# DeltaNet and SwiGLU feed-forward on one core: Q turned by VectorE, a merge on four column groups, a planner with transfer lanes

## The chip, the cores and the metric

The kernel runs on one core of a Trainium2 chip. The metric is the device time of one execution in microseconds; the time before is the median of three runs, 712.82 us (711.55 to 713.73).

A core has five engines that run their own instruction streams in order and meet at semaphores: TensorE (PE; its weight loads are listed as PEld), VectorE (DVE), ScalarE (ACT), GpSimd (POOL) and SyncE (SP). SP issues nearly all transfers (DMAs) here, in the order in which they are written; if one has to wait, all behind it wait. Matmuls write to PSUM, eight banks of 128 x 512 fp32.

## The reference

A DeltaNet recurrence over 768 steps with 4 batches x 8 heads of width 48, followed by a normalized SwiGLU feed-forward block on 3072 tokens of width 384. Everything is fp32; the weights of the block arrive as 8-byte floats.

```python
def _attn_ref(q, k, v, beta):              # q, k, v: 4, 8, 768, 48
    k_n = k / (np.linalg.norm(k, axis=-1, keepdims=True) + 1e-06)
    state = np.zeros((B, H, D, D), dtype=np.float32)
    for t in range(S):
        y[:, :, t] = np.einsum('bhd,bhde->bhe', q[:, :, t], state)
        v_old = np.einsum('bhde,bhd->bhe', state, kt)
        state = state + bt[:, :, :, None] * np.einsum('bhd,bhe->bhde', kt, vt - v_old)
...
def _moe_ref(x, w_gate, w_val, w_out, rms_g):   # x: 3072, 384; 1536 hidden
    rms = np.sqrt(np.mean(x * x, axis=-1, keepdims=True) + 1e-06)
    xn = x / rms * rms_g
    g = xn @ w_gate
    silu = g * (1.0 / (1.0 + np.exp(-g)))
    val = xn @ w_val
    return silu * val @ w_out
```

## The kernel before

**Chunks.** The 768 steps are cut into 12 chunks of 64 (C). In a chunk the recurrence is written as matmuls: a triangular system of 64 x 64 for each of the 32 pairs of batch and head is inverted, and the inverse is applied to V less what the state predicts. The inverse is made as two halves of 32 (W), which are then merged. After that the 256 tokens of the chunk go through the feed-forward block.

**The work on one chunk c**, by function and line:

- `load` (493): transfers of K, Q and V into `k2`, `q2` and `vt`. Q comes as two transfers, one for each parity g of the head, each 64 steps x 16 heads x 48 numbers. `q2` is a single buffer of 128 x 16 x 64, of which 48 columns are loaded and 16 are zero; it is filled again for the next chunk once the turn has read it.
- `norms` (551): the lengths of K's rows (line 557 on VectorE, line 560 on GpSimd).
- `prep` (583): K is scaled (629) and turned (`turn`, 508: eight transposes on TensorE, line 515, and two copies out of PSUM, line 525 or 527); K's scores (`scores`, 529, matmul at line 538) are copied (637), sent to DRAM and back in another layout (`dkk`, `at_`), scaled (654), and the two half inverses are built in 15 steps on VectorE (701 and 707). They go to DRAM and back (`dx`, `dxt`; into `mt`, `x2bd`, `m1bd`), and two merges on TensorE make the block that joins the halves: `merge1` (780, matmul at 783) and `merge2` (802, matmul at 807). The copies out of the second merge (821 on ScalarE, in chunk 0 one at 823 on VectorE) complete `mt`.
- `qpart` (568): Q is turned in the same way into `qt`, Q's scores against K are made (538) and masked into `pt` (578).
- `recur` (826): the state is applied to K and Q (848), `mt` to the rest of V (894), then `pt` (908) and K (945) to the result; the outcome is normalized and turned (1016, 1020) into `xf` for the feed-forward block. The new state is added at line 1047.
- The feed-forward block: for chunks 0 and 1 `ffn_plain` (1072; gate and value matmuls at 1083, down at 1065), in halves of the hidden width, since the weights are still arriving. From chunk 2 on `ffn` (1163) with 15 products of blocks in the place of 18 (1176) whose weights are sums made once by `factors` (1129) and `out_factors` (1202), and `down` (1214, matmul at 1233). VectorE adds products at 1186, ScalarE copies them at 1188 and takes SiLU at 1192, VectorE multiplies at 1193.

**The weights** come as 8-byte floats in 18 transfers through three buffers and are converted on ScalarE (465) and VectorE (453, 456, 461, 486); three of them are summed on TensorE (478, 479).

**The second merge** writes eight products of a 128 x 32 weight with a 128 x 128 moving tile. In the code before, the half batch bb picks the column group of the array (rows 0 or 64 of the output) and (g, p) picks 128 columns:

```python
for g in range(2):
    for p in range(2):
        for bb in range(2):
            x_ = 2 * g + p
            nc.tensor.matmul(
                ps2[bb].t[64 * bb : 64 * bb + W, 128 * x_ : 128 * x_ + 128], ...
```

An fp32 matmul stands as two records in the trace, a transpose as one.

**The order of the work** isn't the order of the code. Every step is handed to a planner (`Plan`, 63) as an operation with an engine, an estimated duration, what it reads and writes, a priority from its due time, and the PSUM banks that it takes. `forward` (111) simulates the five engines: among all operations that could start, the one with the earliest start goes first, then the one with the lowest key. A transfer occupies its issuing engine for `dur` and then one shared server for `work`. `backward` (186) makes new keys from the latest start that each operation could have, and `run` (214) repeats both 60 times with small random shifts and keeps the shortest plan, whose order is then written out engine by engine. Until planned time 70 us TensorE's gaps are filled with unneeded matmuls on `ident` (1333). A flag `after` holds a transfer back until a planned time; for Q it is 0.0, 27.2 and, from chunk 2 on, 53.2.

Of the kernel before, what the change touches and what calls it, by code (L numbers as in the profile page):

```python
# [18 lines left out]
C = 64  # L19
W = 32  # L20
# [42 lines left out]
class Plan:  # L63
# [3 lines left out]
    def __init__(self):  # L67
        self.ops, self.wrote, self.read, self.slack, self.lead = [], {}, {}, 0.0, 0.0
        self.rows = 128
        self.late = False  # L70

    def add(self, eng, dur, fn, prio, r=(), w=(), lat=0.15, ps=(), last=(), size=0):
        ps, last = ((t,) if isinstance(t, Group) else tuple(t) for t in (ps, last))
        deps = set()
        for key in r:
            if key in self.wrote:
                deps.add(self.wrote[key])
        for key in w:
            if key in self.wrote:
                deps.add(self.wrote[key])  # L80
            deps.update(self.read.get(key, ()))
        ahead = self.lead if eng == "PE" else 0.0
# [4 lines left out]
        op.size = size  # L87
# [12 lines left out]
        return op  # L100

    def first_priorities(self):
        for op in reversed(self.ops):
            if op.late:
                op.prio = min(
                    (u.prio - (0.0 if u.eng == op.eng and not op.dma else op.lat + u.slack + 0.2) for u in op.users),
                    default=op.prio,
                ) - STRETCH[op.eng] * op.dur - (3.0 if op.dma else 0.0)
            op.key = op.prio - op.ahead

    def forward(self, banks, until):
# [11 lines left out]
        order, server, end_, mode = [], 0.0, 0.0, 0  # L123
        backlog = 0.0
        while len(order) < len(self.ops):
            best = None
            for e in ENGINES:
                for op in cand[e]:
                    s = max(op.at, at[e])
                    if op.port:  # L130
                        s = max(s, held["POOL" if e == "DVE" else "DVE"])
# [41 lines left out]
            if op.dma:  # L173
                server = max(end + 0.9, server) + op.work
                end = server
            op.end = end
            for u in op.users:
# [36 lines left out]
    def run(self, free, filler=None, until=0.0):  # L214
# [4 lines left out]
        for k in range(ROUNDS):  # L219
            order = self.forward([t for t, _ in free], until if filler else 0.0)  # L220
            if order is None:
                break
            self.ends.append(self.end)
            if best is None or self.end < best[0]:
                best = self.end, [(op, op.start) for op in order]
            self.backward()
            for op in self.ops:
                op.key += SHAKE * (k % 3) * rng.uniform(-1.0, 1.0)
        self.end = best[0]
# [20 lines left out]
def kernel(  # L250
# [57 lines left out]
    k2 = sbt("k2", [128, 16, DP], NK)  # L308
    q2 = sbt("q2", [128, 16, DP])
    vt = sbt("vt", [128, 16, D])  # L310
    ksum = sbt("ksum", [128, 16], 2)
# [53 lines left out]
    def dma(dst, src, prio, r=(), w=(), work=0.3, dur=0.5, eng="SP", after=0.0):  # L365
        queue = nc.scalar if eng == "ACT" else nc.sync
        op = P.add(eng, dur, lambda: queue.dma_start(out=dst, in_=src), prio, r, w, lat=0.7)
        op.dma, op.work, op.ready = True, work, after

# [7 lines left out]
    def setup():  # L377
# [32 lines left out]
        for i in range(2):  # L410
            P.add("POOL", 1.0, lambda t=mt[i]: nc.gpsimd.memset(t, 0.0), 1, w=[("mt", i, h_, bb) for h_ in range(3) for bb in range(2)] + [("mt", i, h_, bb, g) for h_ in range(2) for bb in range(2) for g in range(2)])

# [80 lines left out]
    def load(c, what):  # L493
        t0 = c * C
        pk, pq, pv = ((-5, 1, 12), (5, 29, 36))[c] if c < 2 else (due(c, 150), due(c, 99), due(c, 70))
        for key, t, src, pr in (("k2", k2[c % NK], k, pk), ("q2", q2, q, pq)):
            for g in range(2):
                if key[0] not in what:
                    continue
                dst = t[64 * g : 64 * g + 64, :, 0:D]  # L500
                s = src.rearrange("b (y g) t e -> g t (b y) e", g=2)[g, t0 : t0 + C]
                dma(dst, s, pr, w=[(key, c % NK if key == "k2" else 0, g)], dur=0.7, work=1.02, eng="ACT" if c == 0 and g and key == "k2" else "SP", after=((0.0, 1.4, 0.0), (8.6, 27.2, 0.0))[c]["kqv".index(key[0])] if c < 2 else 53.2)
        if "v" in what:
# [79 lines left out]
    def prep(c):  # L583
# [210 lines left out]
        else:  # L794
# [4 lines left out]
            ), pi, r=[ps1], w=[("yn", 0)], last=ps1)  # L799
        ps2 = [Group(), Group()]  # L800

        def merge2():
            for g in range(2):
                for p in range(2):
                    for bb in range(2):
                        x_ = 2 * g + p
                        nc.tensor.matmul(  # L807
                            ps2[bb].t[64 * bb : 64 * bb + W, 128 * x_ : 128 * x_ + 128],
                            zz[:, 2 * bb + p, g],
                            x2bd[:, 4 * g + 2 * bb + p].rearrange("p y t -> p (y t)"),  # L810
                        )

        P.rows = 32
        P.add("PE", 0.9, merge2, pi, r=[("yn", 0)] + [("x2bd", y_) for y_ in range(4)], w=ps2 + [("mt", imt, 2, bb) for bb in range(2)], ps=ps2, size=32)
        P.rows = 128
        for bb in range(2):
            s = slice(64 * bb, 64 * bb + W)
            dst = mt[imt][s, :, W:C]
            src = lambda s=s, bb=bb: ps2[bb].t[s].rearrange("p (x t) -> p x t", t=W)
            if c or bb:  # L820
                P.add("ACT", A(512), lambda dst=dst, s=src: nc.scalar.copy(dst, s()), pi, r=[ps2[bb]], w=[("mt", imt, 2, bb)], last=ps2[bb])
            else:
                P.add("DVE", V(512), lambda dst=dst, s=src: nc.vector.tensor_copy(out=dst, in_=s()), pi, r=[ps2[bb]], w=[("mt", imt, 2, bb)], last=ps2[bb])


    def recur(c):
# [6 lines left out]
        sk = [("st", g) for g in range(2)]  # L833
        mtk = [("mt", imt, i, bb, g) for i in range(2) for bb in range(2) for g in range(2)] + [("mt", imt, 2, bb) for bb in range(2)]
        ptk = [("pt", d) for d in range(2)]
# [236 lines left out]
    def ffn_plain(c, f0, f1, start):  # L1072
# [3 lines left out]
        def up(f):  # L1076
            ps = Group()
            h_, i_, n = f // 6, f % 6 // 2, 128 * (f % 2)
            for side, key in enumerate(("wg", "wv")):
# [7 lines left out]

                P.add("PE", 1.31, mm, start + 3.9 * (f - f0), r=xk + [("wuse", h_)] + ready[(key, h_, i_)], w=[ps, (("sil", f % 2), ("hf", f, 0))[side]], ps=ps, size=12)
            a = f % 2
# [3 lines left out]
        def down(f):  # L1093
            if f == f0:
                P.add("PE", 0.0, lambda: None, start, r=xk + [("cvp", n, x_) for n in range(NPE) for x_ in range(2)], w=["po"], ps=po[1])
            P.add("PE", 1.31, down_mm(po, f, f0, f1), start + 3.9 * (f - f0) + 9, r=[("hf", f, 0), ("hf", f, 1), "wouse"] + ready[("wo", f)], w=["po"], ps=po[0], size=8)
# [66 lines left out]
    def ffn(c, start):  # L1163
        n = 0
        for h in range(2):
            ps = [Group() for _ in range(3)]
            for m, ((kind, slot), xs, b_, begin, o, more_, end) in enumerate(PRODUCTS):
# [13 lines left out]
                first = ["acq"] if m < 3 else []  # L1181
                P.add("PE", 0.9, mm, start + 0.95 * n, r=["xc", ("xp", 0), ("xp", 1), ("wx", h)], w=[g] + first, ps=g, size=16)
                n += 1
# [18 lines left out]
    def out_factors():  # L1202
        b = lambda i, j: wo_sb[:, 6 * i : 6 * i + 6, 192 * j : 192 * j + 192]
        wk = [key for f in range(FT) for key in ready[("wo", f)]]
        old = [(n_, i, d) for n_, i in (("kka", 1), ("kkb", 2)) for d in range(2)] + [("xs", 0), ("xs", 1)] + [("mt", 1, h_, bb) for h_ in range(3) for bb in range(2)] + [("mt", 1, h_, bb, g) for h_ in range(2) for bb in range(2) for g in range(2)]
        for n, (dst, in0, in1) in enumerate((
# [80 lines left out]
    load(1, "k")  # L1287
    P.slack, P.lead = 0.0, 1000.0
    norms(0)
    prep(0)  # L1290
    qpart(0)
    norms(1)
    load(1, "q")
    for c in range(NCH):
        for part_ in (recur, prep):
# [5 lines left out]
            else:  # L1301
                P.slack, P.lead = 0.0 if c < 1 else 0.1, 1000.0
                recur(c)
        P.slack, P.late = 1.0, True
        if c + 2 < NCH:
# [63 lines left out]
```

## Time and profile before

| | |
|---|---|
| median of three runs | 712.82 us |
| span of the profiled execution | 709.8 us |
| instructions on TensorE, VectorE, ScalarE, GpSimd | 10040, 1138, 732, 140 |
| second-largest share of the chain of waits: VectorE | 5% |
| bytes moved | 54.66 MB in 210,070 packets |
| filler matmuls, line 1333 | 28.0, 11.6 and 8.3 us by shape |
| Q's transfers | 24, to landing 3.7 us (median) |
| mt's transfers | 84 from SP, 32 KB each, to landing 2.2 us (median) |

The profiled execution's own time isn't recorded beside its span: the span runs from the first to the last instruction of this one execution, and the runs were timed without a profile, so 712.82 - 709.8 = 3.02 us is taken as what lies around it. Durations in the profile are per instruction, in ns for single ones. A matmul's duration is its way through the pipeline, several of which overlap, so what a group takes from TensorE is read from the distance between starts, or from the chain of waits, where each piece ends at the start of the next.

### The profile page before, as it was taken

What the parts mean: (1) busy time and instruction counts of PE and PEld (TensorE: products, weight loads), DVE (VectorE), ACT (ScalarE), POOL (GpSimd) and SP (SyncE); (2) the same over time, 40 slices, a digit from 0 to 9 for tenths busy, and PEclk for the clock granted to TensorE, in tenths of its full rate; (3) what the DMA queues carried; (4) which work ended last, traced back from release to release, by engine and by line L of the source; (5) the groups of instructions that cost most, each with busy time, mean ns of one, the idle gap of its engine ahead of it and who ended that gap; (6) DMA issues with size and microseconds to landing.
All of it is one profiled execution on the core that took longest, in us unless ns stands there. A gap on an engine that the chain in (4) does not pass through costs nothing.

```text
span 709.8 us, 23280 instructions
## 1 busy us (share of the span) xinstructions
PE 700.7 (99%) x10040; PEld 637.8 (90%) x10040; DVE 543.5 (77%) x1138; ACT 314.0 (44%) x732; POOL 139.9 (20%) x140
## 2 busy tenths in 40 slices
PE   8999999999999999999999999999999999999997
PEld 5657868778799999999999999999999999999997
DVE  4899989999679759849969769669679547957373
ACT  5435554233245445445444445346345345245241
POOL 4201211103133132233223133133213003000000
PEclk9999999999999999999999999999999999999999
DMA  7878795341451161162542431442430350040000
GB/s 138 221 149 188 180 262 170 51 79 24 75 112 27 33 111 31 28 111 46 90 77 47 74 71 25 90 76 48 78 67 11 56 103 2 15 64 2 23 1 23
DMA packets 210070, 54.66 MB, mean 77 GB/s; under 512 B 199216, under 2 KB 202288, under 8 KB 209968
## 3 DMA queue, kind: packets, MB, share of 16 engines
q1 hardware_dynamic: 205120, 52.26, 36.9%
q10 hardware_dynamic: 4848, 0.92, 0.8%
q8 instruction: 79, 1.29, 0.8%
q14 instruction: 23, 0.19, 0.1%
HBM read 40.83 MB, written 12.32 MB: 75 GB/s over the span
## 4 chain that ended last, share of the span: by engine, by line
PE 91%; DVE 5%; DMA 3%; issue 1%; ACT 1%; POOL 0%; ACTq 0%; POOLq 0%; DVEq 0%
PE bank L1176 39%; PE bank L1233 19%; PE bank L1083 9%; PE bank L1065 4%; PE bank L538 3%; PE bank L848 3%; PE bank L515 3%; PE bank L1333 2%; PE bank L894 2%; PE bank L908 2%; DMA more<-in_moe_w_gate_dram 2%; PE bank L807 2%; DVE acc L707 1%; PE bank L1016 1%; PE bank L945 1%; DVE acc L701 1%
## 5 line engine op out<-in xcount | busy, mean ns | idle before, releaser
L1186 DVE TENSOR_TENSOR tmp<-tmp,bank 128x512 f32<-128x512 f32 x180 | 121.2, 682 | 79.5 <-PE bank L1176 68.5
L1176 PE MATMUL bank<-xf,w_in 128*128 128x128 f32 x1440 | 181.1, 277 | 0.0
L1176 PEld LDWEIGHTS bank<-xf,w_in 128*128 128x128 f32 x1440 | 170.1, 192 | 2.6 <-issue 0.8
L1176 PE MATMUL bank<-xf,more 128*128 128x128 f32 x960 | 125.2, 277 | 0.0
L1176 PEld LDWEIGHTS bank<-xf,more 128*128 128x128 f32 x960 | 115.4, 192 | 2.4 <-issue 0.6
L1188 ACT COPY tmp<-bank 128x512 f32<-128x512 f32 x120 | 69.0, 586 | 78.2 <-PE bank L1176 58.3
L1192 ACT ACTIVATE tmp<-tmp 128x256 f32<-128x256 f32 x120 | 49.9, 417 | 97.9 <-DVE tmp L1186 97.6
L707 DVE TENSOR_REDUCE acc<-acc 128x30 f32<-128x90 f32 (+4 forms) x180 | 85.1, 473 | 6.2
L560 POOL TENSOR_TENSOR knrm<-ksum,half 128x16 f32<-128x16 f32 x12 | 36.2, 3019 | 158.0 <-DVE ksum L559 158.0
L701 DVE TENSOR_TENSOR acc<-acc,at 128x60 f32<-128x60 f32 (+4 forms) x180 | 62.3, 346 | 2.8
L1233 PE MATMUL bank<-wo_sb,hf 128*128 128x192 f32 x360 | 63.7, 327 | 0.0
L1233 PEld LDWEIGHTS bank<-wo_sb,hf 128*128 128x128 f32 x360 | 58.3, 190 | 0.1
L1193 DVE TENSOR_TENSOR hf<-tmp 128x256 f32<-128x256 f32 x120 | 51.0, 437 | 7.7 <-ACT tmp L1192 7.2
L1333 PE MATMUL bank<-ident 128*128 128x128 f32 (+2 forms) x160 | 44.9, 427 | 1.4 <-POOL ident masks.py:199 1.4
L728 POOL COPY acc<-acc 128x128 f32<-128x128 f32 x40 | 21.5, 568 | 123.1 <-DVE acc L707 122.5
L1333 PEld LDWEIGHTS bank<-ident 128*128 128x128 f32 x160 | 27.0, 196 | 17.9 <-issue 15.2
L654 POOL TENSOR_TENSOR at<-at,beta_b 128x1024 f32<-128x1024 f32 x8 | 18.9, 2360 | 85.7 <-DMA at<-dkk 73.7
L1083 PE MATMUL bank<-xf,w_in 128*128 128x256 f32 x144 | 34.6, 385 | 0.9 <-DVE r L862 0.9
L1065 PE MATMUL bank<-wo_sb,hf 128*128 128x384 f32 x96 | 34.6, 491 | 0.0
L1083 PE MATMUL bank<-xp,w_in 128*128 128x256 f32 x144 | 32.8, 380 | 0.0
L1083 PEld LDWEIGHTS bank<-xf,w_in 128*128 128x128 f32 x144 | 26.4, 190 | 6.0 <-DVE r L862 1.5
L1083 PEld LDWEIGHTS bank<-xp,w_in 128*128 128x128 f32 x144 | 27.0, 190 | 4.6
(166 smaller groups left out, 1024.5 us busy)
## 6 DMA issues: line engine op xcount, KB each, us to landing
at<-dkk SPq DMA_DIRECT2D x23, 256.0 KB, 4.2
q<-in_q_dram SPq DMA_DIRECT2D x24, 192.0 KB, 3.7
more<-in_moe_w_val_dram SPq DMA_DIRECT2D x6, 768.0 KB, 6.2
more<-in_moe_w_gate_dram SPq DMA_DIRECT2D x6, 768.0 KB, 7.4
more<-in_moe_w_out_dram SPq DMA_DIRECT2D x6, 768.0 KB, 6.9
vt<-in_v_dram SPq DMA_DIRECT2D x24, 192.0 KB, 4.2
out_dram<-tmp SPq DMA_DIRECT2D x48, 96.0 KB, 2.2
k<-in_k_dram SPq DMA_DIRECT2D x23, 192.0 KB, 3.8
```

The source lines that it names most:

```text
L560: P.add("POOL", 2.95, lambda: nc.gpsimd.tensor_tensor(out=knrm[i2], in0=ksum[i2], in1=half, op=ALU.pow), pn, r=[("ksum", i2), "half"], w=[ ...
L701: nc.vector.tensor_tensor(out=acc[:, 1:3, 0:n, j + 2 : W].rearrange("p a i t -> p i a t"), in0=acc[:, old, 0:n, j : j + 2, None].to_broadc ...
L707: nc.vector.tensor_reduce(out=acc[:, new, 0:n, j + 2 : W], in_=acc[:, lo : lo + 3, 0:n, j + 2 : W].rearrange("p a i t -> p i t a"), axis=A ...
L1065: nc.tensor.matmul(po[p].t[:, 0:DM], hf[:, spot(f), 128 * p : 128 * p + 128], wo_sb[:, spot(f)], start=(f == f0), stop=(f == f1 - 1), skip ...
L1083: nc.tensor.matmul(ps.t[:, TOK * side : TOK * side + TOK], w_in[:, side, h_, 3 * t + i_, n : n + 128], x_[:, 2 * t : 2 * t + 2].rearrange( ...
L1176: nc.tensor.matmul(g.t[:, 128 * z : 128 * z + 128], fac[:, side, 128 * f : 128 * f + 128], xf[:, xs], start=(begin and z == 0), stop=False ...
L1186: P.add("DVE", V(512), lambda t=t, g=g: nc.vector.tensor_tensor(out=t, in0=t, in1=g.t, op=ALU.add), -1, r=[g], w=[tk], last=g)
L1188: P.add("ACT", A(512), lambda t=t, g=g: nc.scalar.copy(t, g.t), -1, r=[g], w=[tk], last=g)
L1192: P.add("ACT", A(256), lambda t=t: nc.scalar.activation(out=t[:, 0:256], in_=t[:, 0:256], func=ACTF.Silu), -1, w=[tk])
L1193: P.add("DVE", V(256), lambda t=t, f0=f0, p=p: nc.vector.tensor_tensor(out=hf[:, spot(f0) : spot(f0) + 2, 128 * p : 128 * p + 128], in0=t[ ...
L1233: nc.tensor.matmul(g.t[:, 0:192], a_[:, f], b_[:, f], start=(begin and f == 0), stop=(f == 5), skip_group_check=True)
L1333: nc.tensor.matmul(warm[:, 0 : 128 * w_].rearrange("p (w n) -> p w n", n=128), ident, ident[:, None, :].to_broadcast([128, w_, 128]))
```

## The change

1. **Q's turn.** From chunk 2 on, Q is loaded in 16 pieces of 32 steps x 8 heads x 32 (or 16) columns, placed so that a transpose of 32 x 32 blocks gives `qt` at once. One VectorE transpose of 128 x 1024 then takes the place of eight TensorE transposes and two ScalarE copies. The loads keep the `after` time of 53.2 that the two transfers had. Chunks 0 and 1 are as before. Columns that the pieces leave unwritten meet the zero columns of K.
2. **The second merge** writes to four column groups, (bb, g), of one bank, 256 columns each, in the place of two groups of two banks with 512 columns. Four copies of 32 x 256 bring it to `mt` in the place of two of 32 x 512.
3. **The planner.** In its simulation a transfer starts no earlier than 0.7 us after the eighth transfer before it has ended. Operations of chunk 0 (`norms`, `prep`, `recur`) get a key 2000 lower, so that they go first among those that can start at the same time. A key "plain" keeps the factored products behind the last plain gate and value matmuls in the plan.

```diff
@@ class Plan
+            op.key = op.prio - op.ahead - (2000.0 if op.first else 0.0)
...
+        lanes = [0.0] * 8
...
+                    if op.dma:
+                        s = max(s, lanes[0])
...
                 server = max(end + 0.9, server) + op.work
                 end = server
+                lanes = lanes[1:] + [end + 0.7]
...
+                if op.first:
+                    op.key = op.n - 2000.0
@@ buffers
+    q2t = q2.rearrange("p x e -> p (x e)").rearrange("p (u g th e) -> p u g th e", u=8, g=2, th=2)
+    q2k = [("q2", i) for i in range(16)]
@@ def load(c, what)
+        if "q" in what and c > 1:
+            for d, eh, g, th in itertools.product(range(2), repeat=4):
+                e0, e1 = 32 * eh, min(D, 32 * eh + 32)
+                src = q.rearrange("b (yh a) t e -> a t (b yh) e", a=4)[2 * d + g, t0 + 32 * th : t0 + 32 * th + 32, :, e0:e1]
+                r0 = 64 * d + 32 * eh
+                dma(q2t[r0 : r0 + 32, :, g, th, 0 : e1 - e0], src, pq, w=[q2k[8 * d + 4 * eh + 2 * g + th]], work=0.2, after=53.2)
...
-                if key[0] not in what:
+                if key[0] not in what or key == "q2" and c > 1:
@@ def qpart(c)
-        turn(q2, qt, qk, [("q2", 0, 0), ("q2", 0, 1), "q2p"], pr, False)
+        if c < 2:
+            turn(q2, qt, qk, q2k + ["q2p"], pr, False)
+        else:
+            P.add("DVE", V(1024), lambda: nc.vector.transpose(out=qt.rearrange("p u t -> p (u t)"), in_=q2.rearrange("p x e -> p (x e)")), pr, r=q2k + ["q2p"], w=qk)
@@ def prep(c): the second merge
-        ps2 = [Group(), Group()]
+        ps2 = Group()
 
         def merge2():
-            for g in range(2):
-                for p in range(2):
+            for p in range(2):
+                for g in range(2):
                     for bb in range(2):
-                        x_ = 2 * g + p
+                        r0 = 64 * bb + W * g
                         nc.tensor.matmul(
-                            ps2[bb].t[64 * bb : 64 * bb + W, 128 * x_ : 128 * x_ + 128],
+                            ps2.t[r0 : r0 + W, 128 * p : 128 * p + 128],
                             zz[:, 2 * bb + p, g],
                             x2bd[:, 4 * g + 2 * bb + p].rearrange("p y t -> p (y t)"),
                         )
...
         for bb in range(2):
+            for g in range(2):
+                s = slice(64 * bb + W * g, 64 * bb + W * g + W)
+                dst = mt[imt][64 * bb : 64 * bb + W, 8 * g : 8 * g + 8, W:C]
+                src = lambda s=s: ps2.t[s, 0:256].rearrange("p (x t) -> p x t", t=W)
...
@@ def ffn_plain, def ffn: a key that the planner sees
-... w=[ps, (("sil", f % 2), ("hf", f, 0))[side]], ps=ps, size=12)
+... w=[ps, (("sil", f % 2), ("hf", f, 0))[side]] + ["plain"] * (c == 1 and f == FT - 1 and side == 1), ps=ps, size=12)
-... r=["xc", ("xp", 0), ("xp", 1), ("wx", h)], w=[g] + first, ps=g, size=16)
+... r=["xc", ("xp", 0), ("xp", 1), ("wx", h), "plain"], w=[g] + first, ps=g, size=16)
@@ the main program
+    P.first = True
     norms(0)
     prep(0)
+    P.first = False
...
+                P.slack, P.lead, P.first = 0.0 if c < 1 else 0.1, 1000.0, c == 0
                 recur(c)
+                P.first = False
```

More of the change, by code (lines that the diff above doesn't have):

```diff
@@ L69, in __init__ @@
         self.rows = 128
-        self.late = False
+        self.late = self.first = False
     def add(self, eng, dur, fn, prio, r=(), w=(), lat=0.15, ps=(), last=(), size=0):
@@ L86, in add @@
         op.mode = self.rows if eng == "PE" else None
-        op.size = size
+        op.size, op.first = size, self.first
         op.port = eng == "DVE" and not any(isinstance(key, Group) for key in r) or eng == "POOL" and "half" not in r
@@ L108, in first_priorities @@
                 ) - STRETCH[op.eng] * op.dur - (3.0 if op.dma else 0.0)
-            op.key = op.prio - op.ahead
+            op.key = op.prio - op.ahead - (2000.0 if op.first else 0.0)
     def forward(self, banks, until):
@@ L367, in dma @@
         op = P.add(eng, dur, lambda: queue.dma_start(out=dst, in_=src), prio, r, w, lat=0.7)
-        op.dma, op.work, op.ready = True, work, after
+        op.dma, op.work, op.ready, op.port = True, work, after, False
     PERIOD = 51.0
@@ L410, in setup @@
         for i in range(2):
-            P.add("POOL", 1.0, lambda t=mt[i]: nc.gpsimd.memset(t, 0.0), 1, w=[("mt", i, h_, bb) for h_ in range(3) for bb in range(2)] + [("mt", i, h_, bb, g) for h_ in range(2) for bb in range(2) for g in range(2)])
+            P.add("POOL", 1.0, lambda t=mt[i]: nc.gpsimd.memset(t, 0.0), 1, w=[("mt", i, h_, bb, g) for h_ in range(3) for bb in range(2) for g in range(2)])
     def load_small():
@@ L501, in load @@
                 s = src.rearrange("b (y g) t e -> g t (b y) e", g=2)[g, t0 : t0 + C]
-                dma(dst, s, pr, w=[(key, c % NK if key == "k2" else 0, g)], dur=0.7, work=1.02, eng="ACT" if c == 0 and g and key == "k2" else "SP", after=((0.0, 1.4, 0.0), (8.6, 27.2, 0.0))[c]["kqv".index(key[0])] if c < 2 else 53.2)
+                dma(dst, s, pr, w=[(key, c % NK, g)] if key == "k2" else q2k[8 * g : 8 * g + 8], dur=0.7, work=1.02, eng="ACT" if c == 0 and g and key == "k2" else "SP", after=((0.0, 1.4, 0.0), (8.6, 27.2, 0.0))[c]["kqv".index(key[0])] if c < 2 else 53.2)
         if "v" in what:
@@ L813, in prep @@
         P.rows = 32
-        P.add("PE", 0.9, merge2, pi, r=[("yn", 0)] + [("x2bd", y_) for y_ in range(4)], w=ps2 + [("mt", imt, 2, bb) for bb in range(2)], ps=ps2, size=32)
+        P.add("PE", 0.5, merge2, pi, r=[("yn", 0)] + [("x2bd", y_) for y_ in range(4)], w=[ps2] + [("mt", imt, 2, bb, g) for bb in range(2) for g in range(2)], ps=ps2, size=32)
         P.rows = 128
         for bb in range(2):
[L817 to L823, printed above, removed]
+            for g in range(2):
+                s = slice(64 * bb + W * g, 64 * bb + W * g + W)
+                dst = mt[imt][64 * bb : 64 * bb + W, 8 * g : 8 * g + 8, W:C]
+                src = lambda s=s: ps2.t[s, 0:256].rearrange("p (x t) -> p x t", t=W)
+                if c or bb:
+                    P.add("ACT", A(256), lambda dst=dst, s=src: nc.scalar.copy(dst, s()), pi, r=[ps2], w=[("mt", imt, 2, bb, g)], last=ps2)
+                else:
+                    P.add("DVE", V(256), lambda dst=dst, s=src: nc.vector.tensor_copy(out=dst, in_=s()), pi, r=[ps2], w=[("mt", imt, 2, bb, g)], last=ps2)
     def recur(c):
@@ L833, in recur @@
         sk = [("st", g) for g in range(2)]
-        mtk = [("mt", imt, i, bb, g) for i in range(2) for bb in range(2) for g in range(2)] + [("mt", imt, 2, bb) for bb in range(2)]
+        mtk = [("mt", imt, i, bb, g) for i in range(3) for bb in range(2) for g in range(2)]
         ptk = [("pt", d) for d in range(2)]
@@ L1086, in mm @@
                         )
-                P.add("PE", 1.31, mm, start + 3.9 * (f - f0), r=xk + [("wuse", h_)] + ready[(key, h_, i_)], w=[ps, (("sil", f % 2), ("hf", f, 0))[side]], ps=ps, size=12)
+                P.add("PE", 1.31, mm, start + 3.9 * (f - f0), r=xk + [("wuse", h_)] + ready[(key, h_, i_)], w=[ps, (("sil", f % 2), ("hf", f, 0))[side]] + ["plain"] * (c == 1 and f == FT - 1 and side == 1), ps=ps, size=12)
             a = f % 2
@@ L1094, in down @@
             if f == f0:
-                P.add("PE", 0.0, lambda: None, start, r=xk + [("cvp", n, x_) for n in range(NPE) for x_ in range(2)], w=["po"], ps=po[1])
+                P.add("PE", 0.0, lambda: None, start, r=xk + [("cvp", n, x_) for n in range(NPE) for x_ in range(2)], w=["po"] + ["plain"] * (c == 1 and f1 == FT), ps=po[1])
             P.add("PE", 1.31, down_mm(po, f, f0, f1), start + 3.9 * (f - f0) + 9, r=[("hf", f, 0), ("hf", f, 1), "wouse"] + ready[("wo", f)], w=["po"], ps=po[0], size=8)
@@ L1181, in ffn @@
                 first = ["acq"] if m < 3 else []
-                P.add("PE", 0.9, mm, start + 0.95 * n, r=["xc", ("xp", 0), ("xp", 1), ("wx", h)], w=[g] + first, ps=g, size=16)
+                P.add("PE", 0.9, mm, start + 0.95 * n, r=["xc", ("xp", 0), ("xp", 1), ("wx", h), "plain"], w=[g] + first, ps=g, size=16)
                 n += 1
@@ L1204, in out_factors @@
         wk = [key for f in range(FT) for key in ready[("wo", f)]]
-        old = [(n_, i, d) for n_, i in (("kka", 1), ("kkb", 2)) for d in range(2)] + [("xs", 0), ("xs", 1)] + [("mt", 1, h_, bb) for h_ in range(3) for bb in range(2)] + [("mt", 1, h_, bb, g) for h_ in range(2) for bb in range(2) for g in range(2)]
+        old = [(n_, i, d) for n_, i in (("kka", 1), ("kkb", 2)) for d in range(2)] + [("xs", 0), ("xs", 1)] + [("mt", 1, h_, bb, g) for h_ in range(3) for bb in range(2) for g in range(2)]
         for n, (dst, in0, in1) in enumerate((
@@ L1301 @@
             else:
-                P.slack, P.lead = 0.0 if c < 1 else 0.1, 1000.0
+                P.slack, P.lead, P.first = 0.0 if c < 1 else 0.1, 1000.0, c == 0
                 recur(c)
+                P.first = False
         P.slack, P.late = 1.0, True
```

## The prediction

> **What bounds the kernel now.** I read the page from the top: busy shares, slices, chain; then the busy time by stage, then TensorE's and SP's order of work around the edited lines.
>
> ```profile
> span 709.8 us, 23280 instructions
> PE 700.7 (99%) x10040; PEld 637.8 (90%) x10040; DVE 543.5 (77%) x1138; ACT 314.0 (44%) x732; POOL 139.9 (20%) x140
> ...
> PE 91%; DVE 5%; DMA 3%; issue 1%; ACT 1%; POOL 0%; ACTq 0%; POOLq 0%; DVEq 0%
> ```
>
> TensorE is busy for 99% of the span and holds 91% of the chain of waits. Its 99% includes filler matmuls (line 1333: 28.0, 11.6 and 8.3 us by shape, 47.9 in all), which run only up to about 72 us, so I ask stage by stage. Columns below: stage, its length, then busy us and (instructions) of PE, PEld, DVE, ACT and POOL, granted clock, DMA share, GB/s.
>
> ```profile
> 70.00:110.00 40.00, 39.12 (x632) 30.38 (x631) 35.98 (x58) 24.38 (x53) 9.54 (x5) 1.00 0.94 226
> 110.00:200.00 90.00, 90.00 (x985) 71.58 (x984) 79.00 (x161) 29.58 (x69) 13.81 (x14) 1.00 0.38 75
> ...
> 320.00:440.00 120.00, 119.96 (x2024) 116.11 (x2024) 99.06 (x217) 58.05 (x138) 30.32 (x28) 1.00 0.33 61
> ```
>
> From 110 us to the last products, TensorE never stands idle by more than a few hundredths, at full clock. There a microsecond of TensorE work removed is a microsecond off the end, as long as nothing else becomes late. The stage 70 to 110 is different: TensorE is nearly full (0.88 us idle), but the DMA engines are 94% and VectorE 90% busy, loading and converting the weights. It is the one place where an added transfer or an added VectorE instruction has little cover.
>
> The last part of the span is a tail of products and stores that the change doesn't touch. The median, 712.82, is 3.02 above this execution's span of 709.8; I carry that difference over unchanged.
>
> **The change, part by part.**
>
> *The turn of Q.* The columns of the first two rows are line, engine, operation, count, busy us and mean ns; the others are start, duration, instruction.
>
> ```profile
> L515 PE MATMUL bank<-ident,q 128*128 128x128 f32 x96 | 14.2, 276 | 0.0
> L807 PE MATMUL bank<-x2bd,yn 128*32 128x128 f32 x192 | 12.9, 276 | 0.0
> ```
> ```profile
> 364.59 0.65 PE L783 MATMUL bank<-m1bd,kk 128*32 128x64 f32 x32
> 365.17 2.05 PE L1176 MATMUL bank<-xf,more 128*128 128x128 f32 x16
> 367.15 1.07 PE L807 MATMUL bank<-x2bd,yn 128*32 128x128 f32 x16
> 368.15 1.16 PE L1176 MATMUL bank<-xf,w_in 128*128 128x128 f32 x8
> ```
>
> Each chunk has 8 transposes of Q, 96 over 12 chunks. A mean of 276 ns is their latency in the pipeline; what they take from TensorE is the distance to the next instruction. In the chain of waits, a group of 4 stands as 0.44 us (381.88 to 382.32) and 8 of K as 0.87 (336.45 to 337.32). So a chunk's Q costs 0.87 us. Chunks 2 to 11 lose it, 10 x 0.87 = 8.7 us; all ten lie after 75 us, where TensorE is full. Two ScalarE copies of 128x512 go with each (line 527, 587 ns), 11.7 us in all off an engine that is 44% busy: worth nothing in itself.
>
> In their place VectorE turns 128x1024 in one instruction. No row shows a VectorE transpose. Its dearest neighbour per element is the strided product of line 679 (128x512 in 1.12 us), which gives 2.24 us for 1024; its cheapest is the shift of line 453 (128x768 in 0.55), which gives 0.74. I take the plain product of the same 128x1024 shape (line 654 on VectorE, 1.22 us), since both stream 1024 elements from SBUF to SBUF: 10 x 1.22 = 12.2 us, between 7.4 and 22.4. VectorE's idle time hides it: of the 494 us from 200 to 694 it is busy 368 (91.57 + 99.06 + 93.62 + 83.74 by stage), so 126 are free and about ten go. Without that cover the whole 12.2 would be on the path. Queued behind the new instruction are VectorE's additions into the product sums (line 1186); these are late by at most 1.2 us once a chunk, and their banks then come free later. Before 200 us two turns (chunks 2 and 3) add 2.4 us to a VectorE that has 15 us left in 70 to 200. The page Vector Engine (DVE) Microarchitecture Reference of the Trainium skill, section 5.2, gives 1.0417 ns a column and about 75 ns an instruction; by it the estimate is 1.14 us a turn and 11.4 in all. No run here shows it yet.
>
> *The loads of Q.* Two transfers of 1024 packets (192 bytes) become sixteen of 256 packets (128 bytes for the first 32 columns, 64 for the other 16). The nearest row has just this form: a transfer into mt, 32 partitions x 8 x 32 numbers, 32 KB.
>
> ```profile
> 339.74 1.31 SPq L367 DMA_DIRECT2D q<-in_q_dram  x2
> ...
> 362.31 5.52 SPq L367 DMA_DIRECT2D mt<-dx  x8
> ```
> ```profile
> L367 SPq DMA_DIRECT2D mt<-dx x84: 323/449/1652, 46.4 to 632.6; - x84
> ```
>
> At the median of 449 ns SP issues sixteen in 7.2 us, where the two took 1.31; at the mean of the eight shown (0.69) in 11.0. That is 5.9 to 9.7 us more of SP for a chunk. One period of the steady state is 53.4 us (the products of line 894 start at 215.74 and 642.77, eight periods apart). SP is far from full there: it waits 48.3 us for the copies of K's scores (line 637) between 200 and 440 alone. And Q is loaded a period ahead (right after its turn at 339.1, used at 381.7), so its own lateness is covered by some 40 us. The wait in front of the loads changes its owner only: the tile must have been read by VectorE's turn instead of TensorE's. Queued behind it on SP are the transfers of the next chunk's preparation.
>
> The rule that speaks against this is in DMA: Bandwidth & Descriptors of the Trainium skill, Anatomy of one DMA — SWDGE (gpsimd) path: a fixed cost of about 2.0 us for each transfer, fitted there for transfers from GpSimd. Sixteen one after another would by that estimate make 32 us a chunk, still inside a period. This trace shows eight in flight together: issued in 5.52 us, 2.2 us each to landing.
>
> In packets a chunk's Q goes from 2048 to 4096. Queue 1 moved 205,120 packets in 36.9% of 16 engines' 709.8 us, or 20.4 ns each, so 2048 more cost 2.6 us of all sixteen engines. In the steady state (share 0.33) that is hidden. The loads for chunks 2 and 3 were issued at 57.5 and 85.6 us, in or before the stage with 94%: 5.2 us at most on the path, 0 if the planner moves them past the weights, which the second half of the weights allows (TensorE first uses it at 135.7, its last conversions end near 110). Between the two I take 1.3, half of one load.
>
> *The second merge.* Before, 16 records of 128 columns on two column groups: 1024 columns in series, 1.00 us (367.22 to 368.22 in the chain). After, four groups: 512 columns in series. The first merge is already that: 32 records of 64 columns on four groups, 512 in series, 0.58 us (364.66 to 365.24). Saved 0.42 a chunk, in eleven chunks after 90 us 4.6 us; chunk 0's, at 58.5, lies among fillers. If the groups didn't overlap, 0. One bank fewer is held. The copies out of it go from two of 32x512 (line 821, 574 ns) to four of 32x256 (line 770, 362 ns): 1.15 to 1.45 us of ScalarE, 0.3 later for line 894, which the planner can cover with products. In chunk 0 VectorE's one 0.68 becomes 0.84 (line 772, two).
>
> *The planner.* Eight lanes, the first chunk's precedence and the key "plain" issue nothing. Lanes only delay transfers in the plan's own clock. "plain" holds the factored products until the plain gate and value matmuls are out; before, 32 records of them ran ahead of that point or among the last down matmuls, and on one engine the order of the same work costs nothing while it stays full. Precedence for chunk 0 could advance its rows: its second hop through DRAM takes from 46.2 to 54.2 us behind other transfers, against 2.2 for a transfer alone, and two issues of SP stand 5.43 us there. What it could give is 0 to 5 us, and only if weights and chunk 1 keep up; a reshuffled start could cost as much. I take 0.
>
> **Sum:** -8.7 - 4.6 + 1.3 = -12.0 against the span, 697.8; with the 3.0 outside it, 700.8. Own range from the bounds: a start 5 us earlier gives 695, all 5.2 of the loads 705.
>
> **Rivals.**
>
> *Early loads on the path.* SP issues for 53.9 of the 59.6 us from 42.3 to 101.8, and the DMA share is 0.94 after. For it: that density. Against: the slack in the second half of the weights. Price 5.2 for packets, and up to 28 more issues x 0.449 = 12.6 for SP: 705 to 712; middle 707.
>
> *The start gains.* Chunk 0 first, with loads ordered by real lanes: 5 us, 696. Against: VectorE, 90% busy, sets the pace of the supply.
>
> *The merge gains nothing.* Four groups take turns: 705.4. Against it stands the first merge's 0.58.
>
> *VectorE becomes the bound.* All 12.2 on the path: 713.0. For: in 110 to 200 it is 88% busy. Against: 25% free afterwards.
>
> *SP's order starves the recurrence (slower).* Place: SP between K's scores and the second merge's inputs. The loads stand in order, wait for VectorE's turn, then occupy SP for 7.2 us while the transfers of the next preparation wait. The steps from K's turn to line 894 now take 27.4 (293.3 to 320.7) to 37.7 us (443.0 to 480.7); with the burst 44.9. It decides only from a period of 52.1 on (53.4 less 1.3), so there must be 7 us of waiting besides. One Q load did wait 22.1 us for a turn. At 9.1 us of waiting the period is 54.0, 0.6 over before, and over eight periods 5 us: 718.
>
> **How the numbers follow.** What can be told from no change is 0.3%, 2.1 us: 710.7 to 715.0. Forecast 0.55 (695 to 705); early loads 0.12; start gains 0.08; merge without gain 0.05; VectorE bound 0.07; SP's order 0.13. Faster: 0.55 + 0.08 + 0.05, with 0.10 of the early loads and 0.02 of VectorE, 0.80. Same: 0.02 and 0.05 of these two, 0.07. Slower: 0.13. The time is the likeliest case's, 700.8; the range, 694 to 713, takes in all but SP's order and a start better than its bound.
>
> **What would show it.** Line 515 keeps 16 records of Q and TensorE loses 80; the second merge stands as 0.58 us in the chain; one VectorE transpose a chunk near 1.2 us; the period of line 894 near 52.1; TensorE still without idle time from 110 on. Wrong: gaps on TensorE before line 894 with SP or a transfer named as releaser, line 1083 waiting for line 486 or 453 in 70 to 110, or a second merge of 1.0 us.

## The result, and the profile after

The changed kernel takes 705.88 us (median of 703.95 to 706.46) where the kernel before takes 712.70 in the same session: a ratio of 0.9898, 95% interval 0.9873 to 0.9922, or 6.8 us less. Forecast were 700.8 us and 12.0 less; the time lies inside the range, and some 5 us of the forecast gain are missing. The profiled execution spans 704.1 us against 709.8.

The head of the page after:

```profile
span 704.1 us, 23246 instructions
PE 687.3 (98%) x9956; PEld 623.0 (88%) x9956; DVE 556.3 (79%) x1149; ACT 307.3 (44%) x735; POOL 139.8 (20%) x140
```

TensorE has 84 records fewer (80 of them Q's) and is busy for 13.4 us less. Its fillers (line 1354 now) take 28.4, 10.8 and 8.9 us, 48.1 against 47.9, so the useful work went from 652.8 to 639.2: 13.6 us less, where 13.3 were forecast. Its idle time (span less busy time) went from 9.1 to 16.8, 7.7 us more. That is the whole account: 13.6 - 7.7 - 0.2 = 5.7 us of span.

The stages of the changed kernel show where TensorE now stands idle (columns as before):

```profile
70.00:110.00 40.00, 36.27 (x630) 27.89 (x625) 34.68 (x60) 21.57 (x51) 7.99 (x5) 1.00 0.89 203
110.00:200.00 90.00, 90.00 (x1165) 69.83 (x1155) 83.29 (x167) 34.00 (x81) 19.86 (x18) 1.00 0.50 94
...
320.00:440.00 120.00, 120.00 (x1815) 116.25 (x1817) 93.16 (x199) 58.51 (x142) 29.82 (x29) 1.00 0.36 61
440.00:560.00 120.00, 116.94 (x1872) 113.30 (x1873) 99.78 (x213) 53.85 (x136) 28.17 (x31) 1.00 0.38 63
```

From 70 to 110 us 3.73 us are missing (0.88 before), from 440 to 560 3.06 (none before); outside these rows 2.62 are missing from 40 to 70 (0.87 before) and 1.2 from 560 to 694 (none before). From 110 to 440 TensorE is as full as it was. What it waits for:

```profile
PE bank L1194 <- ACT tmp L1206: 2.5, 1, 2.5
PE bank L926 <- issue: 2.2, 1, 2.2
PE bank L800 <- DVE m1bd L789: 1.5, 2, 0.9
...
PE bank L963 <- issue: 1.1, 1, 1.1
```

These are single events, not one in every chunk. The two edits to the work did what was worked out for them. The merge (line 824 now), the transposes of Q left on TensorE, and VectorE's turn:

```profile
L824 PE MATMUL bank<-x2bd,yn 128*32 128x128 f32 x192 | 7.7, 279 | 0.0
L529 PE MATMUL bank<-ident,q 128*128 128x128 f32 x16 | 2.1, 273 | 0.0
```
```profile
473.54 0.65 PE L824 MATMUL bank<-x2bd,yn 128*32 128x128 f32 x16
474.12 2.94 PE L1194 MATMUL bank<-xf,w_in 128*128 128x128 f32 x24
```
```profile
L589 DVE STREAM_TRANSPOSE qt<-q x10: 1232/1238/1245, 101.5 to 568.8; 128x1024 f32<-128x1024 f32 x10
```

From the merge's start to the next instruction are 0.58 us, as forecast, and its busy time fell from 12.9 to 7.7 us. The turn takes 1.238 us, ten times.

### The profile page after: what moved, and what is told of

It is laid out like the page before. It is cut to its first block, busy times and chain, and to the rows that moved or that the text cites. A ratio compares the mean times of both kernels' runs of the same rounds, so it can differ in the third digit from the quotient of the medians.

```text
span 704.1 us, 23246 instructions
## 1 busy us (share of the span) xinstructions
PE 687.3 (98%) x9956; PEld 623.0 (88%) x9956; DVE 556.3 (79%) x1149; ACT 307.3 (44%) x735; POOL 139.8 (20%) x140
## 5 line engine op out<-in xcount | busy, mean ns | idle before, releaser
L1260 DVE TENSOR_TENSOR tmp<-tmp,bank 128x192 f32<-128x192 f32 x30 | 10.5, 350 | 31.9 <-PE bank L1251 30.8
```

## The experiments

The work theory says that what leaves TensorE comes off the end. Its rivals: the loads of Q cost time in the start stage; the planner's draw (every edit makes it find another order) moves the time by itself. In the table "work" is TensorE's busy time without fillers, "idle" its idle time in the span, "to 110" the part of it up to 110 us; then the time at which the transfers of chunk 1's half inverses (`dx`) are issued and the start of the first gate matmul. The ratio is against the kernel before in the same session. Median and ratio come from all executions of a kernel, the columns from "work" on from one profiled execution, whose time can be off the median: by most in after_s48 (704.55 against 708.88), no_lanes (707.99 against 710.65), m_only (711.74 against 713.76) and no_first (710.21 against 708.21).

| kernel | median us | ratio (95%) | work | idle | to 110 | dx at | gate at |
|---|---|---|---|---|---|---|---|
| before | 712.70 | | 652.8 | 9.1 | 4.7 | 69.8 | 72.1 |
| changed | 705.88 | 0.9898 (0.9873-0.9922) | 639.2 | 16.8 | 8.4 | 71.6 | 73.4 |
| m_only | 713.76 | 1.0011 (0.9988-1.0034) | 648.2 | 13.8 | 6.0 | 70.0 | 74.4 |
| q_only | 716.10 | 1.0054 (1.0034-1.0073) | 648.8 | 20.3 | 13.1 | 74.3 | 72.3 |
| plan_only | 716.01 | 1.0068 (1.0043-1.0092) | 651.9 | 13.6 | 7.9 | 73.0 | 75.2 |
| loads_only | 731.50 | 1.0268 (1.0240-1.0296) | 660.3 | 23.2 | 11.5 | 77.3 | 72.5 |
| loads_lanes | 726.64 | 1.0217 (1.0168-1.0266) | 658.8 | 16.7 | 7.4 | 70.2 | 76.7 |
| no_lanes | 710.65 | 0.9980 (0.9957-1.0002) | 642.9 | 16.0 | 6.8 | 74.8 | 70.2 |
| no_first | 708.21 | 0.9937 (0.9921-0.9954) | 643.9 | 17.3 | 11.0 | 72.0 | 78.7 |
| q_from4 | 704.14 | 0.9886 (0.9863-0.9908) | 642.0 | 12.4 | 7.7 | 70.2 | 72.4 |
| q_hold | 703.00 | 0.9852 (0.9815-0.9890) | 639.3 | 15.4 | 10.0 | 70.2 | 72.3 |
| q_hold_fetch | 708.56 | 0.9920 (0.9896-0.9945) | 642.8 | 16.5 | 8.9 | 69.2 | 70.7 |
| before_s48 | 713.87 | 1.0025 (1.0009-1.0042) | 653.4 | 11.0 | 4.8 | 69.2 | 71.5 |
| after_s48 | 708.88 | 0.9953 (0.9928-0.9978) | 638.2 | 16.2 | 9.0 | 71.6 | 73.6 |

### Each part alone

**m_only**, the second merge alone (the diff's part 2 on the kernel before):

> The kernel before with only the second merge on four column groups. Work theory (what leaves TensorE comes off the end): TensorE's busy time without fillers falls by 5.0 us, the time by 4.6 to about 708, with idle time as before (9 us). Plan-draw theory (any edit makes the planner draw another order, and orders differ by several us): the busy time falls just so, but the idle time moves by 2 us or more either way, 706 to 712. If the four groups take turns, the merge stays at 1.0 us and nothing is gained.

The busy time falls by just the 4.6 us, and the idle time rises by 4.7: nothing is gained, and the median lies above the ranges of both theories. The new idle time is spread over the start, 110 to 200 us and the last stages. The merge itself is 7.7 us busy here too, so its price is right and the order found around it is worse.

**q_only**, Q's turn and loads under the old planner (the diff without `lanes`, `first`, "plain" and the merge):

> The kernel before with only Q's turn on VectorE and its sixteen loads, under the old planner (no lanes, no precedence, no plain key). Work theory: TensorE busy less by 8.7 us without fillers, time about 704. Loads theory (the small loads of chunks 2 and 3 cost 3 to 5 us in the stage up to 110 us): idle time of TensorE from 40 to 110 us 3 us or more above the 1.75 of before, time about 707 to 709. Plan-draw theory: the idle time moves anywhere, also after 200 us.

Slower than before, although 80 records leave TensorE. The stage from 70 to 110 us:

```profile
70.00:110.00 40.00, 30.91 (x549) 24.38 (x542) 30.81 (x49) 17.38 (x40) 5.24 (x3) 0.87 0.83 203
```

9.1 us idle, and the mean clock 0.87. SP issues all sixteen loads of chunk 2 in one go from 57.26 to 72.36, and chunk 1's `dx`, 69.8 before, comes at 74.3. Of the 8.7 us of work removed, 4.0 remain in the busy time. The slower clock accounts for the rest in size: its mean over this execution is 0.993, and 0.7% of 650 us is 4.6.

**loads_only**, the sixteen loads alone; the layout, TensorE's turn and all other work stay as before:

```diff
+        if "q" in what and c > 1:
+            for g, th, xh, eh in itertools.product(range(2), repeat=4):
+                e0, e1, r0 = 32 * eh, min(D, 32 * eh + 32), 64 * g + 32 * th
+                src = q.rearrange("b (y g) t e -> g t (b y) e", g=2)[g, t0 + 32 * th : t0 + 32 * th + 32, 8 * xh : 8 * xh + 8, e0:e1]
+                dma(q2[r0 : r0 + 32, 8 * xh : 8 * xh + 8, e0:e1], src, pq, w=[q2k[8 * g + 4 * th + 2 * xh + eh]], work=0.2, after=53.2)
```

> The kernel before with Q from chunk 2 on loaded in sixteen pieces of the same sizes (128 and 64 byte packets), but into the old layout and still turned by TensorE; old merge and old planner. Hidden-loads theory: TensorE's work as before, time within 1.5 us of before. Loads theory: 3 to 5 us slower, 716 to 718, the idle time in 40 to 110 us. SP theory: later still, 718 and more, with TensorE waiting in the steady state for line 894's inputs.

19 us slower. SP's order of issue, and TensorE's waits that followed (columns: start, us, instruction):

```profile
57.48 15.79 SPq L368 DMA_DIRECT2D q<-in_q_dram  x16
...
77.31 2.14 SPq L368 DMA_DIRECT2D dx<-wsum  x2
```
```profile
88.14 1.86 PE L765 MATMUL bank<-ident,wsum 32*32 32x32 f32 x64 [4.96 <-DMA wsum<-dx]
114.78 1.96 PE L914 MATMUL bank<-u,pt 64*64 64x48 f32 x64 [5.05 <-DVE u L939]
```

In the kernel before, the two loads stand at the same place, and the transfers back (`wsum<-dx`) go out at 75.54, where they go out at 82.10 here:

```profile
57.52 6.43 SPq L367 DMA_DIRECT2D q<-in_q_dram  x2
75.54 1.81 SPq L367 DMA_DIRECT2D wsum<-dx  x4
```

Sixteen issues hold SP for 15.8 us, the two held it for 6.43. In both kernels the first issue alone takes nearly 6 us (5.82 and 5.65); the other fifteen here have the median of 0.45 us that the prediction took. So the sixteen cost SP 9.4 us more, inside the 5.9 to 9.7 of the prediction. Chunk 1's `dx` stands behind them and goes out 7.5 us later than before; TensorE then waits 4.96 us for what comes back. For that wait the mechanism is shown: it is the price of an in-order queue, not only of packets. For the 19 us it isn't. Of these, 14.1 are added idle time (4.8 of it from 110 to 200 us) and 7.5 added busy time, at a mean clock of 0.87 from 70 to 110 us and 0.96 from 110 to 200, less 0.9 of fillers; they were not followed back one by one.

**plan_only**, the planner's changes alone:

> The kernel before with only the planner's changes (lanes, chunk 0 first, plain key); Q by TensorE and two loads, old merge. Work theory: no work is removed, 712 to 714. Start theory (precedence gives up to 5 us): 708 to 711, with chunk 0's line of mt products before 61 us. Plan-draw theory: 709 to 716.

Slower by 0.7%: the first gate matmul comes at 75.2 instead of 72.1, chunk 1's `dx` 3.2 us later. Neither the work theory nor the start theory holds here.

So each part alone gives nothing or loses. All three together gain 6.8 us.

### Parts taken away from the changed kernel

**no_lanes** (the two lines with `lanes[0]` out of `forward`) and **no_first** (`P.first` never set):

> The changed kernel without the eight lanes in the planner; everything else as changed. Lanes theory (without them the plan places the sixteen loads too early, and the queue in front of the weights and of chunk 1's transfers grows): TensorE idle 8 us or more more than the changed kernel's 6.4 in 0 to 110 us, granted clock below 1.00 there, time 712 to 722. Plan-draw theory: 700 to 712, idle time anywhere.

> The changed kernel without the precedence of chunk 0. If precedence gives something at the start: chunk 0's first gate matmul later than the changed kernel's 73.4 us and 2 us or more slower, 708 to 711. If it costs (it pushes chunk 1 and the weights back): first gate matmul near 72, idle time from 40 to 110 us below 5, 702 to 705. Plan-draw theory: a move of up to 4 us either way, also after 200 us.

Without lanes 4.8 us are lost, without precedence 2.3. Another seed alone costs the changed kernel 3.0 (after_s48, below): the 4.8 exceed the one redraw that was tried, the 2.3 don't, and the interval of no_first meets that of the changed kernel. In both runs the idle time hardly differs from the changed kernel's (16.0 and 17.3 against 16.8), and the busy time for the same work is longer (642.9 and 643.9 against 639.2), at a lower clock.

In no_lanes thirteen loads of Q go out in one go (56.6 to 69.2), and chunk 1's `dx` at 74.8. The idle time up to 110 us did not grow, against the expectation (its 6.4 us is the changed kernel's figure from 40 to 110 us; from 0 it is 8.4); what grew is the slow clock (0.96 and 0.98 in the stages from 70 to 200) and waits from 110 to 200 (1.9 us). In the changed kernel V's and K's loads come in between:

```profile
59.82 3.37 SPq L375 DMA_DIRECT2D q<-in_q_dram  x7
64.74 1.32 SPq L375 DMA_DIRECT2D vt<-in_v_dram  x2
66.11 1.80 SPq L375 DMA_DIRECT2D q<-in_q_dram  x3
68.03 2.37 SPq L375 DMA_DIRECT2D k<-in_k_dram  x2
...
71.62 1.26 SPq L375 DMA_DIRECT2D dx<-wsum  x2
```

In no_first a load of K for a later chunk stands ahead of chunk 0's last transfers:

```profile
52.85 0.30 SPq L375 DMA_DIRECT2D x2bd<-dx  x1
55.98 1.36 SPq L375 DMA_DIRECT2D k<-in_k_dram  x2
57.38 0.81 SPq L375 DMA_DIRECT2D x2bd<-dx  x1
58.23 0.94 SPq L375 DMA_DIRECT2D mt<-dx  x2
```

and the first gate matmul, 73.4 in the changed kernel, comes at 78.7; the clock from 70 to 110 us is 0.91. Precedence doesn't advance the start against the kernel before (72.1); it keeps other chunks' transfers, K's here, from delaying it.

**loads_lanes**, loads_only with the lanes added:

> The kernel before with Q in sixteen small pieces in the old layout, turned by TensorE, as in loads_only (731.5 us), but with the eight lanes in the planner. Lanes theory (the plan without lanes puts the loads where the queue is full; with them it spreads them): most of the 19 us comes back, 712 to 718, idle time of TensorE from 70 to 200 us below 5 (12.2 in loads_only), clock 1.00. If the loads themselves cost, whatever the plan: 725 and more.

Only 4.9 of the 19 us come back, so the lanes theory is too strong. Chunk 1's `dx` begins to be issued at 70.2 again, but its two issues take 4.7 us (1.9 before), and the transfers back go out 4.7 us later than before:

```profile
70.17 4.68 SPq L372 DMA_DIRECT2D dx<-wsum  x2
80.27 1.84 SPq L372 DMA_DIRECT2D wsum<-dx  x4
```

The first gate matmul is 4.6 us late (76.7), and 5.3 us of idle time lie after 200 us. The sixteen loads still went out together, from 54.8 to 67.7. That lanes alone suffice is refuted; that the loads cost time whenever they are placed is not shown, since the preparation's transfers still come late; how much of the rest is the want of precedence was not tried on this kernel.

### Do the early loads explain what is missing?

**q_from4** leaves chunks 2 and 3 with two loads and TensorE's turn; **q_hold** keeps all work and holds chunk 2's loads back in the plan:

```diff
-  dma(q2t[r0 : r0 + 32, :, g, th, 0 : e1 - e0], src, pq, ..., work=0.2, after=53.2)
+  dma(q2t[r0 : r0 + 32, :, g, th, 0 : e1 - e0], src, pq, ..., work=0.2, after=105.0 if c == 2 else 53.2)
```

> The changed kernel with chunks 2 and 3 still loaded by two transfers and turned by TensorE; VectorE turns from chunk 4 on. TensorE's work rises by 1.7 us, but no small load of Q falls into the stage up to 110 us. Early-loads theory: idle time from 40 to 110 us falls from 6.4 back towards 1.8, time about 703 (701 to 704). Plan-draw theory: the idle time from 40 to 110 stays at 4 to 6 us, time 705 to 710.

> The changed kernel with chunk 2's sixteen loads of Q held to planned time 105 us (53.2 before); all the same work. Early-loads theory: the transfers that were at 60 to 90 us leave the full stage, TensorE's idle time from 40 to 110 us falls from 6.4 to about 3, its stalls without a named wait in that stage (3.3 us) fall below 1.5, time about 702. If the idle time there has another cause (the order of chunk 0 and 1, the draw of the plan), it stays at 5 to 7 us and the time at 704 to 709.

Both are the fastest medians, 704.1 and 703.0, and near what the early-loads theory said; but not for its reason. The idle time up to 110 us is 7.7 and 10.0, where the changed kernel has 8.4 and the theory expected some 3 to 5 us less. What improved is the idle time after 110 us: 0.4 and 1.4 (up to 10 us before the span's end) in the place of 4.2. In q_hold, with no load of Q in the stage, the stall without a named wait even grew:

```profile
98.97 1.13 PE L926 MATMUL bank<-u,pt 64*64 64x48 f32 x59
103.59 0.32 PE L926 MATMUL bank<-u,pt 64*64 64x48 f32 x5 [3.48 <-issue]
103.84 4.54 PE L1101 MATMUL bank<-xf,w_in 128*128 128x256 f32 x12
```

As the cause of the idle time up to 110 us the early loads are refuted. Each of these edits also makes the planner draw another order, so what brings their 1.7 and 2.9 us isn't shown. Q_hold is the fastest kernel measured; its interval meets the changed kernel's at 0.9873 to 0.9890, so the two are not clearly apart.

**q_hold_fetch** asks what that stall is: after 59 of 64 records with nothing to wait for. The planner is told that TensorE's instructions arrive more slowly in that stage (`FETCH0` 34 for 42):

> q_hold (703.0 us) with one number of the planner changed: the rate at which it believes TensorE's instructions arrive while the weights load, 34 a microsecond in the place of 42, so that it spaces the dense groups of small matmuls in that stage. Instruction-supply theory (the stalls of 3.5 and 1.4 us without a named wait come from more records in a short time than arrive while the DMA engines are full): these stalls fall below 2 us in all up to 130 us, TensorE's clock there back to 1.00, time 700 to 702. If the stalls come from something else: they stay at 4 to 5 us, time 702 to 705. Plan-draw: the idle time after 200 us may move by 3 us either way.

The stalls without a named wait are gone up to 130 us (4.9 us in q_hold, none of 0.2 or more listed). The time is worse by 5.6 us all the same: the new order waits for copies to `m1bd` (2.9 us at 88.5), for `yn` (2.0 at 109.0), and the clock is 0.96 in two stages. That denser groups of small matmuls meet the stall is supported by this one run; a remedy it is not.

### The draw

**before_s48** and **after_s48**: another seed for the random shifts, the same work (`random.Random(48)`).

> The kernel before with another seed for the planner's random shifts (48 in the place of 47); the same work in another drawn order. Work theory: 711 to 715. Plan-draw theory: a move of 3 us or more, 716 to 722, if the order of before is a lucky draw.

> The changed kernel with seed 48; the same work in another drawn order. Work theory: 704 to 707. Plan-draw theory: 3 us or more off 705.9, either way (699 to 712); TensorE's busy time without fillers stays at 639 us, all of the move in its idle time.

The seed moves the time by 1.9 us (against 711.97 in that session) and by 3.0 us, each time to the slower side. The executions of after_s48 lie between 704.6 and 713.1, a far wider spread than the kernel's with seed 47 (703.95 to 706.46). The granted clock goes with it: its mean over the execution is 1.000 in the shortest and 0.992 in three of the four longest (710.27, 712.22, 713.09); 0.8% of 705 us is 5.6. In q_hold the one execution at 1.000 took 699.37 us, the other three, at 0.995 to 0.997, 702.29 to 703.94. So one and the same order meets the slow clock in one execution and not in the next, and a median also tells how often; what decides it was not found.

## Why the prediction was right, and what it mis-sized

The time lies inside the stated range, 694 to 713, and the mechanism, work taken off a full TensorE, is what the changed kernel's profile shows, though no part alone does. But the likeliest case's own bounds were 695 to 705; 705.88 lies just above them, where the rival "Early loads on the path" begins (705 to 712). That the range held owes something to its width.

- **The bound** was read rightly: TensorE sets the end, and the work removed can be added up from the distances between starts. 13.3 us forecast, 13.6 measured. The merge (0.58 us a chunk) and VectorE's turn (1.22 taken, 1.238 measured) hit their rows.
- **VectorE's cover** held for the turn: VectorE's busy time rose by 12.8 us, and from 110 to 440 us TensorE has no gap.
- **The start** was mis-sized: 1.3 us were taken "for half of one load"; idle time up to 110 us rose by 3.75. The first gate matmul is 1.3 us later, and two stalls without a named wait (2.2 and 1.1 us) are new. Loads of Q are not needed for the larger one (q_hold has 3.5).
- **After 110 us nothing was taken, and 4.1 us were lost.** The largest event is the 2.5 us at 455.7, shown in the last section; it belongs to this order. Q_from4 and plan_only have 0.4 and 0.0 there from 200 us on.
- **The step that failed** is the sentence on the planner, "I take 0". It priced the three edits, but not the reordering that each of them causes. The kernel before has the least idle time of all fourteen orders measured, 9.1 us; the others have 11.0 to 23.2, and 11.0 is the same work with another seed. So 7.7 us of new idle time stand where the sum has 1.3. And lanes and precedence, costed at nothing, are worth 4.8 and 2.3 us here, the second no more than a redraw.
- **The offset**: 3.0 us around the span were carried over; the profiled execution of the changed kernel took 705.78 for a span of 704.1, so 1.7. With 1.7 the span of 709.8 belongs to an execution of 711.5, which is the lowest of the four measured (711.55), and 1.3 us of the median's difference weren't overhead.
- **The signs.** Line 515's 16 records of Q, the 0.58 us of the merge and the turn near 1.2 us came; "TensorE still without idle time from 110 on" did not. Nor did a period near 52.1: between the same two groups of line 894 (912 now) it is 55.5 (192.93 to 637.26), because the planner moved the first of them 22.8 us forward and the last 5.5. The distance between two groups is no measure of the pace where a planner places them.
- **Two readings were off.** "Eight in flight together" is not in the rows: of the eight transfers issued within 5.52 us, five at most are under way at once. And SP's 53.9 us of issuing are rows of several issues with the waits between them; the issues alone add up to 46.7.
- **The rivals**: "The merge gains nothing" and "VectorE becomes the bound" are refuted. "The start gains" too: the start is later. "SP's order starves the recurrence" has its mechanism right and its place wrong: SP's sixteen issues do delay the next preparation's transfers, in the start stage, by 7.5 us under the old planner (loads_only, 19 us slower in all). "Early loads on the path" named that stage and bounded it at 12.6 us for SP; in loads_only it is 16.4 (9.4 for chunk 2's loads, 7.0 for chunk 3's).

What stays open: why the planner's changes alone are slower than the old ones, how the 19 us of loads_only come about beyond the one wait, what lets an order meet the slow clock, and how much of the remaining idle time another draw would remove.

## What to carry to other kernels

In a kernel whose order a planner finds, take the work removed from the full engine as the most that can be gained (13.3 us here, of which 6.8 came); compare the idle time of the old order with that of other draws first, because every edit here gave up some of what the old order had. Sixteen small transfers in the place of two are a question of the issuing queue and of what stands behind it, not of bytes: price the issues one by one, and look at what waits behind the last of them. Look at the granted clock of every execution before putting a few microseconds down to an edit. And test an edit together with the scheduling that it needs: alone, none of these parts gained anything here.

## What the runs showed of the hardware

**A gap can cost more than its length, and its length doesn't tell when.** In ten-microsecond stages the granted clock stayed at 1.00 in the changed kernel through gaps of 2.2 us (at 101) and 2.5 us (at 455.7). After the 3.5 us of q_hold it is 0.83 from 100 to 110: twelve gate records take 4.54 us there, against 2.86 for the same twelve in the changed kernel (103.41 to 106.27). In q_only an idle stretch of 8.3 us ends at 88.2; the clock is 0.74 from 80 to 90 and 0.75 from 90 to 100. But shorter gaps were followed by a slow clock too. In q_from4 no gap from 100 to 110 us is longer than 0.9 us (three of them, 1.6 in all, between groups of small matmuls), and the clock is 0.83:

```profile
100.00:110.00 10.00, 8.39 (x141) 5.08 (x140) 8.43 (x14) 4.19 (x10) 2.36 (x2) 0.83 0.97 180
```

In no_lanes it is 0.83 from 110 to 120 with gaps of 1.2 and 1.3 us; in plan_only, after a stall of 2.27 us that ends at 66.4, it is 0.50 from 67.3 to 70.7. These runs give no length of gap from which the clock falls.

**TensorE can stall without a named wait while the DMA engines are full.** The stall of q_hold begins after 59 of 64 records at 100.1 us; from 98 to 104 us queue 1 alone holds the DMA engines for more than the whole stretch, and the instruction queue has one packet in those six microseconds, found between 101 and 102. The rows of these two answers (queue: packets, MB, share):

```profile
q1 hardware_dynamic: 1522, 1.35, 108.6%
q8 instruction: 1, 0.02, 1.2%
```

That TensorE had run out of instructions, and that the packet with the next ones waited behind the others, is the likely reading; it wasn't measured by itself.

**VectorE stands still beside GpSimd.** In the changed kernel (VectorE, GpSimd, ScalarE, TensorE):

```profile
450.65 5.72 DVE L1053 TENSOR_TENSOR xf<-xf 128x128 f32<-128x128 f32 x6
```
```profile
451.82 2.52 POOL L671 TENSOR_TENSOR at<-at,beta_b 128x1024 f32<-128x1024 f32 x1 [3.20 <-DMA at<-dkk]
454.48 1.74 POOL L696 TENSOR_TENSOR acc<-at 128x512 f32<-128x512 f32 x1
```
```profile
457.61 1.56 ACT L1206 COPY tmp<-bank 128x512 f32<-128x512 f32 x3 [8.10 <-DVE tmp L1260]
```
```profile
458.25 1.16 PE L1194 MATMUL bank<-xf,w_in 128*128 128x128 f32 x8 [2.51 <-ACT tmp L1206]
```

Six additions that take 2.46 us together in the kernel before take 5.72; the fifth lasts 2.57 us, beside GpSimd's instruction of 2.52, and the sixth 1.82, beside the next one of 1.74. ScalarE then waits for VectorE, and TensorE for ScalarE. The Trainium skill (SBUF — State Buffer, section SBUF: two separate sides) describes an exclusive lock on the port pair that the two engines share, held for a whole instruction when the VectorE operation reads two SBUF inputs; these rows agree. The planner has a rule for it too, but GpSimd's start depends on when a transfer lands (it waited 3.20 us for `at<-dkk`); where the plan had it isn't shown.
